# A second written order for the later batches, a shorter gate, fused score exponentials and key pooling, and one store for the last tokens

## The chip, the cores and the metric

The kernel runs on one core of a Trainium2 chip. The metric is device time in microseconds (us), from runs of the whole program. Engines go by their names in the profile: PE is TensorE (PEld its weight loads), DVE is VectorE, ACT is ScalarE, POOL is GpSimd, SP is SyncE.

## The reference

Eight batches of 576 tokens go through two layers. The first is attention with 8 heads of 64, whose keys and values are means over 8 neighbouring tokens, so that there are 72 of each. The second is a mixture of four causal single-head attention experts. A gate takes the two largest of four logits of a token, and the token's output is the sum of those two experts' outputs, weighted by a softmax over the two.

```python
k_p = k.reshape(B, H, Sp, pool, D).mean(axis=3)      # pool = 8
v_p = v.reshape(B, H, Sp, pool, D).mean(axis=3)
scores = scale * np.matmul(q, k_p.transpose(0, 1, 3, 2))
attn = softmax(scores); x = np.matmul(attn, v_p)     # heads joined: (8, 576, 512)
...
logits = x @ w_gate                                  # (8, 576, 4)
topk = np.argpartition(-logits, K, axis=-1)[..., :K] # K = 2
for e in range(E):
    q = x @ wq[e]; k = x @ wk[e]; v = x @ wv[e]
    scores = np.where(causal, -1000000000.0, scale * (q @ k.transpose(0, 2, 1)))
    ye = softmax(scores) @ v @ wo[e]
    out += (gate weight of e, 0 where not chosen) * ye
```

## The kernel before, in words

Every batch goes through the same steps. A batch has four blocks of 128 tokens (c = 0 to 3) and a tail of 64; the tails of two neighbouring batches share block 4. Which instruction stands after which on each engine is written out by hand: the string SEQ is a list of tokens, and a loop at the end of the kernel issues them one after the other (lines 704 to 762). The framework adds the semaphores that the data need, but each engine keeps the order of the list. A token is name, arguments, batch, then "@" and the PSUM banks of a matmul step; an ending "d" puts a copy on DVE instead of ACT, an ending "p" on an output copy (y) leaves its store to a token of its own (zs).

- L_k, L_q, L_v (line 112): loads of the keys, queries and values, cast on the way, issued by POOL: three, four and three of a batch (batch 0 differs). Each tensor has three raw buffers (NRAW), used in turn.
- PK, kc, kt: the key pooling on PE (line 265), its transpose on DVE, a copy. PV and vc: the value pooling and its copy. u0, u1: transposes of q on DVE.
- E and e: scores of the pooled attention and their exponentials (ACT). D, d, x: the sum over keys, its logarithm, and the exponential of minus that, so the reciprocal. O and o: the weighted values and their scaling on DVE, which makes x.
- V and v: values and gate logits of the experts. g (line 397): the gate, ten steps, the first on ACT and the others on DVE: the exponentials Ex; maximum and minimum of pairs (hi, lo), from these the second largest logit m2 (s2, s3, m2); a mask of the logits that reach it; W = Ex times mask; the sum of W, its reciprocal, and the weights G.
- P and p: projections to queries and keys (P_t: those of the tail) and copies. S and s (line 490): expert scores and their exponentials on ACT, in four tiles (ti 0 to 3); ti 3 holds the last keys, for which line 496 issues two ACTIVATEs, one for each expert of a pair. a: the causal mask, an affine_select on POOL.
- B, then bz, bg, b: weighted values, a reciprocal, the gate weight, and a scaling into osc, all three on DVE. T and t: transposes on PE and copies; in batches 2 to 5 the token F takes their place, a crossbar transpose by DMA, issued by SP.
- Y and y (line 602): the output projection and its copy from PSUM to one of nine ofin buffers. z (line 617): the store to HBM; block 4 goes in two pieces of 64 rows, and for the last batch one piece is issued by SP, the other by ACT. The very last block is copied in two halves, ya on ACT and yb on DVE.
- H: matmuls on zeros that keep PE busy early on.

SP thus holds stores and crossbar transposes in one queue, and POOL loads and masks in one.

Of the kernel before, what the change touches and what calls it, by code (L numbers as in the profile page):

```python
# [8 lines left out]
FP32 = mybir.dt.float32  # L9
# [7 lines left out]
ISEQ = mybir.AluOpType.is_equal  # L17
EXP = mybir.ActivationFunctionType.Exp
# [3 lines left out]
def kernel(  # L22
# [37 lines left out]
    HALF = TPP // 2  # L60

# [335 lines left out]
    def gate(b, step):  # L397
# [14 lines left out]
        elif step == 1:  # L412
            L2 = L.rearrange("p c (a b) -> p c a b", b=2)
            for nm, op in (("hi", MAXOP), ("lo", MINOP)):
                nc.vector.tensor_tensor(
                    out=tmp(nm, 2, 1), in0=L2[:, :, :, 0:1], in1=L2[:, :, :, 1:2], op=op
                )
        elif step == 2:
            for nm, src, op in (("s2", "hi", MINOP), ("s3", "lo", MAXOP)):
                nc.vector.tensor_tensor(  # L420
                    out=tmp(nm, 1), in0=got(src)[:, :, 0, :], in1=got(src)[:, :, 1, :], op=op
                )
        elif step == 3:
            nc.vector.tensor_tensor(
                out=tmp("m2", 1), in0=got("s2"), in1=got("s3"), op=MAXOP
            )
        elif step == 4:
            nc.vector.tensor_tensor(
                out=tmp("msk", E), in0=L, in1=got("m2").to_broadcast([128, n, E]), op=ISGE
            )  # L430
        elif step == 5:
            nc.vector.tensor_mul(out=tmp("W", E), in0=got("Ex"), in1=got("msk"))
        elif step == 6:
# [3 lines left out]
        elif step == 7:  # L437
# [4 lines left out]
        elif step == 8:  # L442
# [47 lines left out]
    def sb(b, bank, dve, ep, ti):  # L490
# [4 lines left out]
        if ti == 3:  # L495
            for e in range(2):
                nc.scalar.activation(
                    out=et[half(b), :, e, eo : eo + n],
                    in_=psum[half(b), bank + e, 0 : 2 * n].rearrange("p (a n) -> p a n", a=NEP),
                    func=EXP, scale=MOE_EXP_SCALE,  # L500
                )
# [288 lines left out]
```

## Time and profile before

| | |
|---|---|
| median of 3 runs | 154.38 us (154.3 to 154.83) |
| profiled execution | span 152.5 us from the first to the last instruction; the page gives no other time of it |
| instructions of the span | 5419 |
| busy time | PE 140.5 us (92%), DVE 125.9 (83%), ACT 135.1 (89%), POOL 89.5 (59%) |
| DMA | 26.67 MB, mean 175 GB/s |
| HBM | read 30.42 MB, written 9.44 MB |
| granted TensorE clock | 0.997 |

Busy time is the share of the span in which an engine had an instruction under way; matmuls are pipelined, and the ends that the profile gives them are modelled. Groups of instructions are read as line, engine, operation, out<-in, shapes, count, then busy time, mean ns of one, and the idle time ahead of them. A line can be that of a helper: L221 is every matmul, L212 every copy. "(+1 forms)" tells that a group mixes shapes. Rows in order of time begin with start and length in us.

### The profile page before, as it was taken

The numbers are of one execution on the slowest core, as the hardware profiler recorded it, in microseconds if no ns is written. First come the engines' busy times: TensorE is split into PE (matmuls) and PEld (weight loads), VectorE is DVE, ScalarE is ACT, GpSimd is POOL, SyncE is SP. The second block draws the span as 40 slices with busy tenths as digits, with TensorE's granted clock in tenths as the row PEclk, the third lists the DMA queues.
The fourth block names the chain that finished last, engine by engine and source line by source line (L and its number), as shares of the span: only waits on it lengthen the run. The fifth ranks groups of instructions, "written<-read, shape, count | busy, mean of one in ns | idle before, by whom it ended". The sixth has DMA issues, their size and how long they took to land.

```text
span 152.5 us, 5419 instructions
## 1 busy us (share of the span) xinstructions
PE 140.5 (92%) x2101; PEld 78.8 (52%) x2122; DVE 125.9 (83%) x415; ACT 135.1 (89%) x247; POOL 89.5 (59%) x161
## 2 busy tenths in 40 slices
PE   6776998999999999999999999999999999999970
PEld 2323353465554465565546655856356667546640
DVE  1784846899899899899989999999897699888960
ACT  3359479999999999999999999999999899999860
POOL 6998588999688979958998171123300344442300
PEclk9999999999999999999999999999999999999998
DMA  4999999999999999999999931536528241389994
GB/s 126 237 186 181 181 179 178 180 180 181 179 188 180 179 181 182 178 180 182 169 173 176 181 34 39 211 84 208 176 92 325 83 121 25 66 282 306 333 340 134
DMA packets 68890, 26.67 MB, mean 175 GB/s; under 512 B 62720, under 2 KB 64000, under 8 KB 68864
## 3 DMA queue, kind: packets, MB, share of 16 engines
q0 software_dynamic: 57408, 14.72, 97.2%
q1 hardware_dynamic: 11088, 10.88, 22.2%
q10 hardware_dynamic: 368, 0.72, 1.5%
q8 instruction: 16, 0.26, 0.6%
q14 instruction: 10, 0.08, 0.2%
HBM read 30.42 MB, written 9.44 MB: 261 GB/s over the span
## 4 chain that ended last, share of the span: by engine, by line
PE 66%; DVE 11%; DMA 10%; POOL 4%; ACT 3%; issue 2%; DVEq 0%; POOLq 0%
PE psum L221 65%; DMA qraw<-in_q_dram 5%; DMA wst_q<-in_moe_wq_dram 4%; DVE xT L377 4%; ACT etb L503 2%; POOL kraw L126 2%; POOL vraw L126 2%; PE psum L230 1%; DVE qT L298 1%; DVE osc L562 1%; DVE oT L212 1%; POOL qraw L126 1%; DVE vp L212 1%; DVE ofin L212 1%; ACT eta L331 1%
## 5 line engine op out<-in xcount | busy, mean ns | idle before, releaser
L503 ACT ACTIVATE etb<-psum 128x1024 bf16<-128x1024 f32 x48 | 47.2, 1032 | 0.8 <-PE psum L221 0.4
L520 POOL TENSOR_SCALAR_AFFINE_SELECT etb<-etb 128x256 bf16<-128x256 bf16 x64 | 25.7, 412 | 37.2 <-ACT etb L503 36.0
L331 ACT ACTIVATE eta<-psum 96x1024 bf16<-96x1024 f32 (+1 forms) x48 | 36.0, 802 | 1.1 <-PE psum L221 0.4
L221 PEld LDWEIGHTS <-etb 128*128 128x128 bf16 x480 | 18.0, 97 | 6.3 <-issue 3.5
L126 POOL DMA_DIRECT2D qraw<-in_q_dram x30 | 19.7, 662 | 2.5 <-DVE gt L557 0.8
L377 DVE TENSOR_TENSOR xT<-psum,rza 128x512 bf16<-128x512 f32 x32 | 20.2, 681 | 1.0 <-ACT rza L354 0.5
L221 PE MATMUL psum<-wvg,xT 128*128 128x260 bf16 x144 | 20.8, 275 | 0.1
L126 POOL DMA_DIRECT2D kraw<-in_k_dram x25 | 19.0, 765 | 2.3 <-POOLq L774 0.8
L221 PE MATMUL psum<-vaug,etb 128*128 128x65 bf16 x480 | 20.2, 193 | 0.0
L126 POOL DMA_DIRECT2D vraw<-in_v_dram x24 | 18.8, 785 | 2.3 <-PE psum L221 1.4
L221 PE MATMUL psum<-xT,wqp 128*128 128x64 bf16 (+1 forms) x123 | 19.2, 282 | 0.5 <-issue 0.2
L221 PE MATMUL psum<-xT,wkp 128*128 128x64 bf16 (+1 forms) x121 | 18.8, 281 | 0.4
L221 PE MATMUL psum<-wop,oT 128*128 128x512 bf16 (+1 forms) x67 | 17.9, 373 | 0.5 <-DVE oT L212 0.3
L212 DVE CAST qk<-psum 128x512 bf16<-128x512 f32 (+1 forms) x23 | 15.0, 653 | 3.6 <-PE psum L221 3.6
L562 DVE TENSOR_TENSOR osc<-psum,gt 128x256 bf16<-128x256 f32 (+2 forms) x40 | 16.7, 421 | 1.0
L221 PE MATMUL psum<-qk 64*128 64x64 bf16 (+4 forms) x192 | 16.2, 277 | 0.6 <-DVE xT L377 0.2
L221 PEld LDWEIGHTS <-xT 128*128 128x128 bf16 x144 | 12.6, 97 | 6.9 <-issue 3.0
L212 ACT COPY ofin<-psum 128x512 f32<-128x512 f32 (+1 forms) x25 | 14.0, 587 | 1.1 <-PE psum L221 0.9
L298 DVE STREAM_TRANSPOSE qT<-qraw 128x576 f32<-128x576 f32 (+1 forms) x18 | 13.2, 750 | 1.0 <-DMA qraw<-in_q_dram 0.9
L221 PE MATMUL psum<-qT,kpT 32*128 32x64 bf16 (+1 forms) x256 | 12.5, 289 | 1.1 <-DVE qT L298 0.9
L221 PE MATMUL psum<-eta,vp 96*32 96x512 bf16 (+1 forms) x256 | 12.7, 288 | 0.5 <-DVE vp L212 0.5
L221 PEld LDWEIGHTS <-wqp 128*128 128x128 bf16 x128 | 8.4, 97 | 8.4 <-issue 2.3
(79 smaller groups left out, 214.4 us busy)
## 6 DMA issues: line engine op xcount, KB each, us to landing
out_dram<-ofin SPq DMA_DIRECT2D x32, 256.0 KB, 2.9
vraw<-in_v_dram POOLq DMA_DIRECT2D x24, 192.0 KB, 6.7
qraw<-in_q_dram POOLq DMA_DIRECT2D x30, 144.0 KB, 7.0
kraw<-in_k_dram POOLq DMA_DIRECT2D x21, 192.0 KB, 7.5
out_dram<-ofin SPq DMA_DIRECT2D x7, 128.0 KB, 2.4
xT<-in_q_dram ACTq DMA_DIRECT2D x2, 288.0 KB, 4.7
xT<-in_k_dram SPq DMA_DIRECT2D x2, 192.0 KB, 4.9
kraw<-in_k_dram POOLq DMA_DIRECT2D x4, 96.0 KB, 5.2
```

Of the source, the lines that this page charges most:

```text
L126: nc.gpsimd.dma_start(out=dst, in_=src)
L212: (nc.vector.tensor_copy if dve else nc.scalar.copy)(out=out, in_=in_)
L221: nc.tensor.matmul(out=out, lhsT=lhsT, rhs=rhs, start=start, stop=stop)
L230: nc.tensor.transpose(out=out[s], in_=in_[:, s], identity=ident[0:n, 0:n])
L298: nc.vector.transpose(out=dst.rearrange("p (a s n) -> p a n s", s=32, n=n)[:, :, own], in_=src.rearrange("p (a n d) -> p a n d", n=n, d=32 ...
L331: nc.scalar.activation(out=dst, in_=src, func=EXP, scale=ATT_EXP_SCALE)
L377: nc.vector.tensor_tensor(out=xT[:, 2 * got[0][0] + t : 2 * got[-1][0] + t + 1 : 2, m + got[0][1].start : m + got[0][1].stop], in0=psum[:, ...
L503: nc.scalar.activation(out=et[:, ep, :, eo : eo + n], in_=psum[:, bank : bank + 2, 0:n], func=EXP, scale=MOE_EXP_SCALE,)
L520: nc.gpsimd.affine_select(out=blk, in_=blk, pattern=[[0, 2], [1, 128]], compare_op=ISGE, fill=0.0, base=0, channel_multiplier=-1,)
L562: nc.vector.tensor_tensor(out=osc(b, ep)[:, own, :].rearrange("p c (e d) -> p e c d", e=2), in0=o[:, :, :, 0:HD], in1=gt.to_broadcast([128 ...
```

## The change

- **Order.** From the pooled-attention scores of batch 1 on (behind the tokens E0:1 and c4:0d) all of SEQ is replaced. It has the same steps of the matrices, in another order, with other banks, and other copies carry the "d". Loads, masks, stores and crossbar transposes stand at other places in POOL's and SP's queues.
- **Gate.** Step 1 compares every logit with every other (ahead, in bf16), step 2 counts how many are larger (c1), step 3 keeps Ex where fewer than 1.5 are larger. The rest is as before, so the gate has eight steps.
- **Key pooling.** Other than in batch 0, one matmul takes the three parts of 128 columns together.
- **Score exponentials.** The tile ti 3 has one ACTIVATE for both experts.
- **Last tokens.** A store of block 4 is one transfer of 128 rows from one queue, for all batches; the last store of all, zs4:7, is this one, from SP.

```diff
@@ -15,6 +15,8 @@
 ISGE = mybir.AluOpType.is_ge
 ISLE = mybir.AluOpType.is_le
 ISEQ = mybir.AluOpType.is_equal
+ISGT = mybir.AluOpType.is_gt
+ISLT = mybir.AluOpType.is_lt
 EXP = mybir.ActivationFunctionType.Exp
 LN = mybir.ActivationFunctionType.Ln
 
@@ -58,6 +60,7 @@
     TPP = S // 32
     LONG = (0,)
     HALF = TPP // 2
+    FINAL = 4
 
     DSC = 1.0 / 64.0
 
@@ -265,11 +268,11 @@
     def PK(b, bank, j=None):
         raw = kraws[b % NRAW]
         n = 64 * (own(j).stop - own(j).start)
-        for c in range(3):
+        for cs in [slice(c, c + 1) for c in range(3)] if b in LONG else [slice(0, 3)]:
             for t in range(2):
                 for i in range(4):
-                    mm(psum[32 * i : 32 * i + 32, bank, n * c : n * c + n], poolk[:, :],
-                       raw[:, c, pair(b, i)][:, own(j), t, :], start=(t == 0), stop=(t == 1))
+                    mm(psum[32 * i : 32 * i + 32, bank, n * cs.start : n * cs.stop], poolk[:, :],
+                       raw[:, cs, pair(b, i)][:, :, own(j), t, :], start=(t == 0), stop=(t == 1))
 
     def kc(b, bank, dve, j=None):
         r = slice(2 * own(j).start, 2 * own(j).stop)
@@ -386,7 +389,7 @@
 
     def small(b, nm, *shape):
         if (b // 2, nm) not in at:
-            at[b // 2, nm] = gtp.tile([128, NPC, *shape], FP32, name=nm, tag=nm)
+            at[b // 2, nm] = gtp.tile([128, NPC, *shape], BF16 if nm == "ahead" else FP32, name=nm, tag=nm)
         return at[b // 2, nm]
 
     def vg(b, bank, dve, c):
@@ -410,36 +413,26 @@
         if step == 0:
             nc.scalar.activation(out=tmp("Ex", E), in_=L, func=EXP)
         elif step == 1:
-            L2 = L.rearrange("p c (a b) -> p c a b", b=2)
-            for nm, op in (("hi", MAXOP), ("lo", MINOP)):
-                nc.vector.tensor_tensor(
-                    out=tmp(nm, 2, 1), in0=L2[:, :, :, 0:1], in1=L2[:, :, :, 1:2], op=op
-                )
+            nc.vector.tensor_tensor(
+                out=tmp("ahead", E, E), in0=L.unsqueeze(2).to_broadcast([128, n, E, E]),
+                in1=L.unsqueeze(3).to_broadcast([128, n, E, E]), op=ISGT,
+            )
         elif step == 2:
-            for nm, src, op in (("s2", "hi", MINOP), ("s3", "lo", MAXOP)):
-                nc.vector.tensor_tensor(
-                    out=tmp(nm, 1), in0=got(src)[:, :, 0, :], in1=got(src)[:, :, 1, :], op=op
-                )
+            nc.vector.reduce_sum(out=tmp("c1", E), in_=got("ahead"), axis=mybir.AxisListType.X)
         elif step == 3:
-            nc.vector.tensor_tensor(
-                out=tmp("m2", 1), in0=got("s2"), in1=got("s3"), op=MAXOP
+            nc.vector.scalar_tensor_tensor(
+                out=tmp("W", E), in0=got("c1"), scalar=1.5, in1=got("Ex"), op0=ISLT, op1=MULT,
             )
         elif step == 4:
-            nc.vector.tensor_tensor(
-                out=tmp("msk", E), in0=L, in1=got("m2").to_broadcast([128, n, E]), op=ISGE
-            )
-        elif step == 5:
-            nc.vector.tensor_mul(out=tmp("W", E), in0=got("Ex"), in1=got("msk"))
-        elif step == 6:
             nc.vector.tensor_add(
                 out=tmp("d2", 2), in0=got("W")[:, :, 0:2], in1=got("W")[:, :, 2:4]
             )
-        elif step == 7:
+        elif step == 5:
             nc.vector.scalar_tensor_tensor(
                 out=tmp("den", 1), in0=got("d2")[:, :, 0:1], scalar=1e-9,
                 in1=got("d2")[:, :, 1:2], op0=ADD, op1=ADD,
             )
-        elif step == 8:
+        elif step == 6:
             nc.vector.reciprocal(out=tmp("rden", 1), in_=got("den"))
         else:
             nc.vector.tensor_mul(
@@ -493,12 +486,11 @@
         c, c0, _ = STILES[ti][0]
         eo = EOFF[c] + c0 - 128 * c
         if ti == 3:
-            for e in range(2):
-                nc.scalar.activation(
-                    out=et[half(b), :, e, eo : eo + n],
-                    in_=psum[half(b), bank + e, 0 : 2 * n].rearrange("p (a n) -> p a n", a=NEP),
-                    func=EXP, scale=MOE_EXP_SCALE,
-                )
+            nc.scalar.activation(
+                out=et[half(b), :, :, eo : eo + n].rearrange("p a e n -> p e a n"),
+                in_=psum[half(b), bank : bank + 2, 0 : 2 * n].rearrange("p e (a n) -> p e a n", a=NEP),
+                func=EXP, scale=MOE_EXP_SCALE,
+            )
         else:
             nc.scalar.activation(
                 out=et[:, ep, :, eo : eo + n], in_=psum[:, bank : bank + 2, 0:n],
@@ -591,7 +583,7 @@
 
     def Y(b, bank, c):
         p0 = 128 * place(b, c)
-        last = (b, c) == (B - 1, 4)
+        last = (b, c) == (B - 1, FINAL)
         n = 256 if last else 512
         for ep in range(NEP):
             for n0 in (0, 256) if last else (0,):
@@ -601,26 +593,19 @@
 
     def y(b, bank, dve, c, half=None, later=False):
         ofin = at[b, "ofin", c] if (b, "ofin", c) in at else ofp.tile([128, DM], FP32, name="ofin", tag="ofin")
+        at[b, "ofin", c] = ofin
         if half is not None:
             cols = slice(256 * half, 256 * half + 256)
             copy(half == 1, ofin[:, cols], psum[:, bank ^ half, cols])
-            at[b, "ofin", c] = ofin
-            if (b, "half", c) not in at:
-                at[b, "half", c] = True
-                return
         else:
             copy(dve, ofin[:], psum[:, bank, :])
-        at[b, "ofin", c] = ofin
-        if not later:
-            z(b, c, nc.sync)
+            if not later:
+                z(b, c, nc.sync)
 
     def z(b, c, queue):
         ofin = at[b, "ofin", c]
         if c == 4:
-            for h in range(2):
-                (nc.scalar if h and b == B - 1 else queue).dma_start(
-                    out=out[b - 1 + h, MAIN:S, :], in_=ofin[64 * h : 64 * h + 64, :]
-                )
+            queue.dma_start(out=out[b - 1 : b + 1, MAIN:S, :], in_=ofin[:])
         else:
             queue.dma_start(out=out[b, 128 * c : 128 * c + 128, :], in_=ofin[:])
 
@@ SEQ @@
-        H1:0@0c H1:0@0c L_q1:1 H1:0@0c e21:0 e20:0 e11:0 D2:0@4 D0:0@5 L_q2:1 PV:0@6 d0:0 D1:0@7 vc:0d H1:0@0 x0:0
...
-        bg00:0 a10:0 e10:2 b00:0 bg01:0 L_q2:3 b01:0 V0:1@7 e11:2 p_k0:1d a12:0 E0:2@02 v0:1d B10:0@6 L_q3:3 W4:0 e01:2
-        V4:1@4 bz10:0 B11:0@7 bg10:0 L_v0:3 b10:0 e00:2 PV:2@5 v4:1d D1:2@6 bz11:0 L_v1:3 P_k1:1@4 vc:2d d1:2 bg11:0
-        b11:0 x1:2 E2:2@02 L_v2:3 D0:2@6 p_k1:1d e21:2 O11:2@7 O01:2@5 d0:2 O00:2@2 o11:2 O10:2@4 L_k0:4 e20:2 PK:3@3
-        x0:2 o10:2 S03:1@0 S10:1@6 L_k1:4 s03:1 o01:2 s10:1 S01:1@0 o00:2 L_k2:4 V3:1@4 s01:1 kc:3 V1:1@5 L_q0:4 v3:1d
-        S02:1@6 S11:1@2 v1:1 kt:3d S12:1@0 s02:1 L_q1:4 V2:2@4 u1:3 P_q1:2@5 a03:1 u0:3 s11:1 L_q2:4 P_q0:2@6 v2:2d
...
-        s02:6 bz10:5 a10:6 B00:5@0 bg10:5 b10:5 V4:7@1 v2:7 bz00:5 a02:6 s01:6 F11:5 B11:5@6 bg00:5 b00:5 P_t0:7@7
-        bz11:5 v4:7 S12:6@2 bg11:5 g4:6 a01:6 F01:5 p_t0:7 S11:6@4 g5:6 S00:6@0 g6:6 P_k0:7@7 g7:6 s11:6 b11:5 g8:6
-        F00:5 g9:6 Y0:4@6 s00:6 a11:6 p_k0:7d Y1:2@4 B10:6@5 y0:4dp s12:6 F10:5 Y4:3@7 a00:6 bz10:6 V1:7@0 zs0:4 bg10:6
-        y1:2p b10:6 V0:7@6 a12:6 v1:7d y4:3p S00:7@2 zs1:2 v0:7d S01:7@4 S02:7@0 zs4:3 s00:7 B00:6@7 g1:7 P_k1:7@6
...
-        B11:7@3 y3:6p t10:7d Y2:6@6 b01:7 bz11:7 zs3:6 T12:6@2 Y1:7@7 bg11:7 y2:6p b11:7 Y0:7@5 t12:6 y1:7dp T01:7@3
-        zs2:6 T11:7@6 B12:7@2 t01:7d t11:7 T02:6@4 B02:7@0 zs1:7 y0:7p bz12:7 Y2:7@3 bg12:7 bz02:7 t02:6 bg02:7 Y3:7@1
-        zs0:7 b02:7 y2:7p b12:7 T02:7@0 y3:7p T12:7@2 t02:7d zs2:7 t12:7d Y4:7@2 zs3:7 ya4:7 yb4:7d
...
+        H1:0@0c H1:0@0c L_q1:1 H1:0@0c e21:0 e20:0 e11:0 D2:0@4 D0:0@5 L_q2:1 PV:0@6 d0:0 D1:0@7 vc:0d H1:0@0 x0:0 c0:0d
...
+        a01:0 s11:0 L_v1:2 kc:2 kt:2 V2:1@1 L_v2:2 o20:1 s12:0 a11:0 p_q0:1 P_q1:1@6 u1:2 a10:0 p_q1:1 E1:2@24 bz01:0
+        v2:1d P_t0:1@1 L_k2:3 u0:2 g6:0 g7:0 p_t0:1d a12:0 e10:2 bg01:0 P_k0:1@6 E0:2@02 L_k1:3 e11:2 b01:0 B11:0@7
+        e01:2 p_k0:1d bz11:0 V0:1@4 B00:0@6 bg11:0 B10:0@5 b11:0 L_k2:4 L_q3:3 bz10:0 L_q0:3 D1:2@2 bg10:0 L_q2:3 e00:2
+        bz00:0 L_v0:3 PV:2@3 d1:2 v0:1d bg00:0 V4:1@7 vc:2 b10:0 v4:1d P_k1:1@0 L_q1:3 b00:0 x1:2 E2:2@24 e20:2 O11:2@7
+        e21:2 p_k1:1d o11:2 D0:2@6 PK:3@1 d0:2 O00:2@0 x0:2 kc:3 O10:2@4 S03:1@2 L_v1:3 s03:1 L_k0:4 S10:1@6 V1:1@5
+        o10:2 o00:2 a03:0 S11:1@2 s10:1 v1:1d O01:2@4 S12:1@0 S01:1@6 o01:2 L_k1:4 V3:1@5 s11:1 L_q1:4 kt:3d L_q0:4
+        P_q1:2@4 v3:1d g1:1 s12:1 L_v2:3 S02:1@2 p_q1:2d g2:1 a11:1 S00:1@0 a10:1 s01:1 u0:3 L_q2:4 V2:2@5 v2:2d
...
+        F01:4 B00:5@0 F00:4 bz11:5 bg11:5 Y2:2@1 B01:5@6 b11:5 s02:6 a01:6 p_t0:7d bz00:5 bg00:5 V2:7@7 b00:5 a10:5
+        a10:6 y2:2p S00:6@4 F10:4 s00:6 S11:6@2 s11:6 F11:4 S12:6@0 s12:6 a11:5 zs2:3 v2:7d a11:6 g5:6 a03:6 F01:5
+        P_k0:7@7 bz01:5 bg01:5 b01:5 F00:5 g6:6 V3:7@6 Y0:2@4 p_k0:7d v3:7d Y1:4@5 S01:7@6 S00:7@2 S02:7@0 s01:7 s00:7
+        y0:2dp y1:4dp s02:7 a01:7 zs0:2 zs1:3 g7:6 a02:7 a00:7 zs1:4 B10:5@4 P_k1:7@5 Y1:2@6 bz10:5 bg10:5 b10:5 p_k1:7d
+        B10:6@4 V0:7@7 S11:7@2 s11:7 S10:7@0 s10:7 Y2:4@5 bz10:6 bg10:6 v0:7d b10:6 y1:2dp F11:5 y2:4dp Y4:3@7 V1:7@4
...
+        bg11:7 y2:6p bg01:7 b11:7 y3:6p B02:7@0 T11:7@3 zs2:6 b01:7 bz02:7 zs3:6 Y1:7@5 t11:7 T01:7@2 B12:7@1 bg02:7
+        b02:7 Y0:7@3 t01:7d T02:6@2 y1:7p zs1:7 y0:7p T12:6@0 bz12:7 bg12:7 b12:7 Y2:7@5 t12:6d T02:7@4 T12:7@1 t02:6d
+        t12:7d t02:7d y2:7p Y3:7@7 y3:7p zs0:7 Y4:7@0 ya4:7 zs2:7 zs3:7 yb4:7d zs4:7
```

More of the change, by code (lines that the diff above doesn't have):

```diff
@@ L639 @@
+        L_q3:1 d2:0 O00:0@6 d1:0 c1:0d O20:0@5 O01:0@4 o00:0 O10:0@2 x1:0 O11:0@3 o01:0 x2:0 X0:0@0 W2:0 o10:0 X1:0
+        o11:0 X2:0 W3:0 c2:0d X3:0 c3:0d o20:0 P_k0:0@4 L_v0:1 h0:0 P_t0:0@5 p_k0:0d L_v1:1 P_k1:0@3 p_t0:0 L_v2:1
         PK:1@2 p_k1:0 S03:0@0 S00:0@4 kc:1 L_k0:2 S02:0@6 s03:0 s02:0 S01:0@2 kt:1d H1:0@0 L_k1:2 H1:0@0 H1:0@0 s01:0
[L640 to L641 removed]
```

98 lines of the change are left out of this document (46 added, 52 removed).

## The prediction

> **What bounds the kernel now.** I read the page's head and its chain of waits first, then busy time by stage, then what ScalarE waits for, and last the groups of instructions.
>
> ```profile
> span 152.5 us, 5419 instructions
> PE 66%; DVE 11%; DMA 10%; POOL 4%; ACT 3%; issue 2%; DVEq 0%; POOLq 0%
> ```
>
> The span is 152.5 us. The median of the runs is 154.38, so 1.9 us lie around the span; I take that part as unchanged, and every difference below counts in full on the median. The chain puts two thirds on TensorE (PE). I don't follow it, for this reason:
>
> ```profile
> 101.06 0.55 PE L221 MATMUL psum<-kraw,poolk 96*32 96x128 bf16 x24
> ```
>
> Twenty-four pooling matmuls take 0.55 us from the first start to the last end. Their modelled durations overlap, so a full PE row does not show a full array. The stages tell more; I cut them at 72 and where batch 7's score exponentials begin (132):
>
> ```profile
> core 0: us, PE busy (x) PEld busy (x) DVE busy (x) ACT busy (x) POOL busy (x), PEclk, DMA share, GB/s
> 25.00:60.00 35.00, 34.09 (x552) 19.02 (x547) 31.40 (x102) 34.16 (x64) 31.09 (x52) 1.00 1.80 181
> 72.00:132.00 60.00, 59.41 (x930) 35.52 (x936) 54.35 (x177) 58.90 (x110) 24.54 (x53) 1.00 0.77 136
> 132.00:148.60 16.60, 15.58 (x198) 9.25 (x199) 14.01 (x62) 14.82 (x29) 4.22 (x11) 1.00 0.87 297
> ```
>
> ```profile
> ACT eta L331 <- PE psum L221: 0.4, 2, 0.3
> ACT etb L503 <- PE psum L221: 0.4, 1, 0.4
> ```
>
> The columns are length, then busy time of PE, weight loads, DVE (VectorE), ACT (ScalarE), POOL (GpSimd). ACT is busy 58.90 of 60 us, and the second fence, its waits from 30 to 140 us, adds up to 0.8 us. DVE stands at 54.35 of 60, nine tenths. In the first row DMA moves a flat 181 GB/s: the input loads run without a break there, and compute can't get ahead of them. So ACT's instruction list sets the time from 72 to 132, the loads stand close to it before, and in the last 16.6 us ACT (14.82) and DVE (14.01) both have air, because the work there is a chain of small handovers.
>
> The Trainium skill, "Trainium Kernel Development and Optimization", Performance Expectations, says that matmul busy time is a bad metric for nearness to the roofline, since matmuls are pipelined. The 24 matmuls in 0.55 us agree. Had I taken the chain at its word, PE would be the bound and the change worth nothing, which is a rival below.
>
> **The change: ScalarE.** Counting tokens with and without the "d" over the whole list, ACT gives away net four output copies (y), two full and two tail query/key copies (p), two wide and three narrow transposed copies (t), and takes two value copies (vc). One pooled-key copy given and one value copy pair taken about cancel and are left out.
>
> ```profile
> L212 ACT COPY ofin<-psum 128x512 f32<-128x512 f32 x24 | 13.6, 596 | 0.6 <-PE psum L221 0.4 <-ACT oT L212 0.2
> L212 ACT CAST qk<-psum 128x512 bf16<-128x512 f32 x10 | 5.8, 590 | 0.5 <-PE psum L221 0.5
> L212 ACT CAST qk<-psum 128x256 bf16<-128x256 f32 x5 | 2.0, 408 | 0.3 <-PE psum L221 0.3
> L212 ACT COPY oT<-psum 128x256 bf16<-128x256 bf16 x5 | 1.9, 388 | 0.4 <-PE psum L230 0.4
> L212 ACT COPY oT<-psum 128x64 bf16<-128x64 bf16 x4 | 0.9, 218 | 0.0
> L212 ACT CAST vp<-psum 96x512 bf16<-96x512 f32 x3 | 1.7, 575 | 0.1
> L497 ACT ACTIVATE etb<-psum 64x128 bf16<-64x128 f32 x16 | 3.5, 271 | 0.1
> L331 ACT ACTIVATE eta<-psum 96x256 bf16<-96x256 f32 x16 | 5.3, 376 | 0.1
> 139.19 1.57 ACT L212 COPY ofin<-psum 128x512 f32<-128x512 f32 x3
> 140.79 0.44 ACT L497 ACTIVATE etb<-psum 64x128 bf16<-64x128 f32 x2
> ```
>
> By durations: 4 x 0.596 + 2 x 0.590 + 2 x 0.408 + 2 x 0.388 + 3 x 0.218 = 5.8 us out, 2 x 0.575 = 1.15 in, so 4.65 less. Neighbours overlap: three copies of 0.596 lie in 1.57, 0.11 saved at each joint. Eleven instructions fewer are eleven joints fewer, 1.2 us, which leaves 3.45. Then the last-key score tile (ti 3): two instructions together took 0.44; one of 256 elements took 0.376 in the pooled attention. That is 0.06 saved seven times (batch 0's lies ahead of the new order), 0.45. The sum for ACT is **-3.9 us**. Since it hardly waits, nothing of its own hides this; what can hide it are DVE, the loads and the end.
>
> **VectorE.** DVE takes what ACT gives, and loses gate steps.
>
> ```profile
> L212 DVE COPY ofin<-psum 128x512 f32<-128x512 f32 (+1 forms) x12 | 7.7, 662 | 0.8 <-PE psum L221 0.7
> L212 DVE CAST qk<-psum 128x512 bf16<-128x512 f32 (+1 forms) x23 | 15.0, 653 | 3.6 <-PE psum L221 3.6
> L212 DVE COPY oT<-psum 128x256 bf16<-128x256 bf16 (+1 forms) x15 | 3.8, 256 | 0.3 <-PE psum L230 0.2
> L212 DVE CAST vp<-psum 96x512 bf16<-96x512 f32 x5 | 3.4, 676 | 2.1 <-PE psum L221 2.0
> L415 DVE TENSOR_TENSOR hi<-L 128x8 f32<-128x8 f32 (+1 forms) x8 | 1.6, 200 | 0.2
> L415 DVE TENSOR_TENSOR lo<-L 128x8 f32<-128x8 f32 (+1 forms) x8 | 1.5, 189 | 0.0
> L420 DVE TENSOR_TENSOR s<-hi 128x4 f32<-128x4 f32 (+1 forms) x8 | 1.3, 156 | 0.0
> L424 DVE TENSOR_TENSOR m<-s,s 128x4 f32<-128x4 f32 (+1 forms) x8 | 1.7, 214 | 0.2
> L428 DVE TENSOR_TENSOR msk<-L,m 128x16 f32<-128x16 f32 (+1 forms) x8 | 1.6, 201 | 0.1
> L562 DVE TENSOR_TENSOR osc<-psum,gt 128x256 bf16<-128x256 f32 (+2 forms) x40 | 16.7, 421 | 1.0
> ```
>
> In: 4 x 0.662 + 4 x 0.653 + 5 x 0.256 - 2 x 0.676 = +5.2. Gate, per batch: hi 0.200, lo 0.189, two s of 0.156, m 0.214, msk 0.201 go, 1.12 us; the step that makes W keeps its place. One compare over 64 or 80 elements ("ahead") and one reduction of it (c1) come. The trace has no such compare and no reduction. From below the s row bounds each (0.156), from above the scaling of 256 elements and more (0.421); I take 0.22, near the m row, whose size is the nearest. So 1.12 - 0.44 = 0.68 per batch, 5.4 in eight, and by the two ends 6.4 or 2.2. DVE comes out at -0.2, with ends at -1.2 and +3.0. It isn't relieved: 54.35 of work into 60 less ACT's gain is some 96% instead of 91%. I price the thinner cover at nothing where the work is spread, and it widens the range by 1.5 us.
>
> For the reduction the Trainium skill speaks against the change: "VectorE: DVE Perf Modes", Rules for kernel authors, calls tensor_reduce the slowest DVE operation and advises to restructure it away; with that page's fitted 151 fixed cycles (section on the TRN2 errata) 80 elements would be an estimated 0.24 us. By that the sum would be 0.3 us worse over 16 instructions, all of it on DVE; no run here shows it.
>
> **TensorE.** The pooling of keys becomes 8 matmuls of 384 columns instead of 24 of 128, four strips side by side as before. The columns are the same, and the row above has all 24 in 0.55 us, so the gain lies between 0 and about 0.2 us a batch, beside ACT work: nothing.
>
> **The end.** From batch 7's first score exponentials (token S01:7) on, the old list has 18 stores, the new one 23 and two crossbar transposes, all on SP's queue; DVE has two output copies, two transposed copies and two osc more. So work has been pushed late.
>
> ```profile
> DMA packets 3757, 5.49 MB, mean 268 GB/s; under 512 B 1192, under 2 KB 1192, under 8 KB 3752
> GB/s 140 11 214 32 340 384 356 232 240 384 356 304 220 240 324 328 348 400 348 368 376 228 336 308 316 384 212 392 380 344 312 336 388 316 76 192 252 0 0 0
> out_dram<-ofin SPq DMA_DIRECT2D x17, 256.0 KB, 2.9
> out_dram<-ofin SPq DMA_DIRECT2D x5, 128.0 KB, 2.4
> ```
>
> This is DMA from 132 us to the end. Five stores of 0.262 MB more make 6.8 MB; at 384 GB/s, which the best slices hold, 17.7 us, against the 16.6 of that stretch. On DVE 2 x 0.662 + 2 x 0.256 + 2 x 0.421 = 2.7 come on top of 14.01: 16.7 of 16.6. Both say about **+1.0**: the tail gets fuller and about one us longer. It could be 0 if the stores keep pace, or 3 if they fall in behind the transposes, which wait for osc with every later store queued behind them on SP. The last transfer is whole, 256 KB, where two halves went out by SP and ACT together; by the last two rows 2.9 against 2.4, part of it queueing, so +0.5 at most and I take **+0.3**. Its wait for both halves of the copy is the old one.
>
> **The sum:** -3.9 + 1.0 + 0.3 = -2.6; 154.4 - 2.6 = **151.8 us**.
>
> **The loads** are the one thing that the order moves ahead of ACT.
>
> ```profile
> DMA  4999999999999999999999931536528241389994
> qraw<-in_q_dram POOLq DMA_DIRECT2D x30, 144.0 KB, 7.0
> vraw<-in_v_dram POOLq DMA_DIRECT2D x24, 192.0 KB, 6.7
> 37.90 0.66 POOL L126 DMA_DIRECT2D qraw<-in_q_dram  x1
> 46.49 1.42 DVE L298 STREAM_TRANSPOSE qT<-qraw 128x576 f32<-128x576 f32 x2
> ```
>
> The first row is DMA in 40 slices of 3.8 us: full in slices 2 to 23, until 88 us. At 181 GB/s a q load (0.147 MB) needs 0.8 us, a k or v load (0.197 MB) 1.1. In the old order batch 3's last q load is issued at 37.90 and lands 7.0 later, about 44.9; its transposes start at 46.49. In the new order one k load of batch 4 and one v load stand ahead of batch 3's last q load, 2.2 us: it lands about 47.1, 0.6 after the old use. DVE is in order, so what waits behind u0:3 waits too. I leave this out of the sum, since the transposes also stand slightly later among ACT's work, and the gain can still be made after 72 us, when the loads are ahead.
>
> **Rivals.** (1) *The end costs nothing.* For it: before, ACT and DVE have air from 132 on, and stores still arrive at 300 to 400 GB/s. Then -3.9 and the 0.2 from DVE: 150.3 us.
> (2) *Another engine is the bound.* PE is busy 59.41 of 60, its array work unchanged, and DVE goes to 96%. If either has no room, ACT's relief turns into waiting: 154.4 less 0.2, 154.2. Against it: the overlapping matmuls, and a gate that is shorter.
> (3) *Slower: the loads run dry.* Loads in the new list are reordered within and across batches, with masks between them on POOL, and the first use of batch 3's q has lost its 1.6 us. Where a late use holds a raw buffer, the next load into it is issued later, DMA idles, and later batches come late too. This adds up: a break of 5% in the 88 us for which the loads run is 4.4 us on top of my sum, 156.2. It decides from 2.6 us of idle DMA on, seen as a rate below 181 in the first row. Against it: a load lands 7 us after its issue, so some six others are queued ahead, a cover that must go first.
> (4) *The gate doesn't get cheaper*, with compare and reduction at 0.421: 3.2 us more on DVE, inside (2).
>
> **The numbers.** My own case gets 0.50, with its own range from 150.5 to 153.4 (the end between 0 and +3 at -3.9 and the cover's 1.5 at one side). Rival 1 gets 0.15, rival 2 0.09, rival 3 0.26, since an order is only as good as the times it was made with, and nothing in this trace shows the new ones. About 0.5%, 0.8 us, is what a measurement of this kernel can tell from no change; the first two cases are faster by more, rival 2 is within, rival 3 slower by more: 0.65, 0.09, 0.26. The range goes from 149.3, rival 1 with DVE at its lower end (-1.2 in place of -0.2), to 156.6, just past rival 3's price; it leaves out the longer breaks of rival 3 and the luckiest ends.
>
> **What would show it.** Right: ACT's busy time down by about 4 us and still 97% and more from 72 us on, DVE at 95%, "ahead" and c1 at 0.2 to 0.25 us, the score exponentials of batch 7 some 3.5 us earlier, a denser store queue at the end, and a last landing about 2.7 us after its issue. Wrong: DMA below 175 GB/s before 85 us or DVE transposes waiting for raw tiles (rival 3); ACT waits of several us put down to DVE or PE (rival 2); last copies done more than 4 us ahead of the end of the span, as stores queue (the end's term too small); a reduction above 0.4 us.

## The result: slower by 8.7%, lost in the last 30 us

| | before | after |
|---|---|---|
| median of 4 runs each, us | 154.36 (154.3 to 154.83) | 167.99 (167.33 to 168.08) |
| ratio | | 1.087 [1.084, 1.090] |
| profiled span, us | 152.5 | 165.8 |
| busy DVE / ACT, us | 125.9 / 135.1 | 122.1 / 132.1 |

The kernel is 13.6 us slower, far past the range. The same views of the kernel after, first the page's head, the chain by engine, and the stages (columns as before: length, PE, PEld, DVE, ACT, POOL, clock, DMA share, GB/s):

```profile
span 165.8 us, 5131 instructions
PE 47%; DMA 24%; POOL 9%; issue 4%; ACT 3%; DVE 3%; SPq 2%; POOLq 0%; DVEq 0%; ACTq 0%
25.00:60.00 35.00, 33.81 (x500) 18.08 (x495) 29.84 (x98) 33.48 (x58) 30.65 (x51) 1.00 1.85 180
60.00:72.00 12.00, 12.00 (x184) 6.61 (x179) 11.47 (x33) 11.06 (x21) 8.56 (x14) 1.00 1.79 191
72.00:132.00 60.00, 59.41 (x906) 34.33 (x905) 51.27 (x160) 57.65 (x100) 24.41 (x52) 1.00 0.82 122
132.00:148.60 16.60, 14.59 (x183) 9.06 (x181) 12.16 (x52) 11.78 (x24) 4.86 (x13) 0.92 0.71 219
```

Up to 132 us little has happened. The loads move 180 GB/s up to 60 us, as before. From 72 us on PE stands at 59.41 of 60, to the hundredth as before, ACT at 57.65 for 58.90, DVE at 51.27 for 54.35. After it everything thins out, DMA too (219 GB/s for 297), and the chain has 24% DMA where it had 10%. DMA from 130 us to the end, in 40 slices of 0.9 us, with the stores issued there (KB each, median us from issue to landing):

```profile
DMA  1549917798399941178998994199941111111100
GB/s 21 115 137 391 366 35 147 272 375 249 39 277 268 282 121 50 53 265 227 286 316 261 316 385 151 50 341 378 355 156 50 50 50 48 50 50 50 50 23 0
out_dram<-ofin SPq DMA_DIRECT2D x23, 256.0 KB, 6.1
```

Look at the right end: eight slices in which DMA is one tenth busy and moves 50 GB/s, an eighth of the 384 that good slices hold. Until 159.5 us a backlog of earlier stores drains there, and then the last store, issued at 155.1, runs alone. The same rate shows in three short stretches before it (39; 50 and 53; 50). Between 157 and 159 us the trace has 49 packets of 2,048 bytes, each 84 ns long: 4.1 us of packet time in 2.0 us, so two packets are under way at a time, and two DMA engines work while fourteen stand still. A store of 256 KB is 128 such packets, 64 for each of two engines, which makes 5.4 us. The waits from 120 us on (us in total, times, longest), the block-4 stores and the landing of all stores, and the chain from 130 us on (start, length) show what this does to the others:

```profile
ACT ofin L215 <- DMA out_dram<-ofin: 5.9, 2, 3.1
DVE ofin L215 <- DMA out_dram<-ofin: 3.5, 1, 3.5
L608 SPq DMA_DIRECT2D out_dram<-ofin x3: 522/557/701, 137.1 to 155.1; - x3
DMA to landing us min/median/max: 2.2/6.1/12.0
137.08 8.31 DMA out_dram<-ofin
145.58 8.81 DMA out_dram<-ofin
154.51 0.42 DVE ofin L215
```

L608 is the block-4 store, three of them here (the fourth, the first in time, was issued at 98 us). Stores issued behind the one of 137.08 land up to 12 us after their issue; that they wait for their share on the same two DMA engines is inferred, as the trace doesn't name a packet's engine. The nine ofin buffers stay held, ACT and DVE wait 9.4 us for one, and the last copy starts at 154.51 instead of 148.2.

### The profile page after: what moved, and what is told of

Same layout as the page of the kernel before. It is cut to its first block, busy times and chain, and to the rows that moved or that the text cites. A ratio compares the mean times of both kernels' runs of the same rounds, so it can differ in the third digit from the quotient of the medians.

```text
span 165.8 us, 5131 instructions
## 1 busy us (share of the span) xinstructions
PE 143.8 (87%) x2010; PEld 78.3 (47%) x2010; DVE 122.1 (74%) x393; ACT 132.1 (80%) x229; POOL 88.5 (53%) x161
## 4 chain that ended last, share of the span: by engine, by line
PE 47%; DMA 24%; POOL 9%; issue 4%; ACT 3%; DVE 3%; SPq 2%; POOLq 0%; DVEq 0%; ACTq 0%
PE psum L224 46%; DMA out_dram<-ofin 10%; DMA qraw<-in_q_dram 9%; POOL kraw L129 3%; DMA kraw<-in_k_dram 3%; POOL qraw L129 3%; DMA oT<-osc 2%; POOL vraw L129 2%; ACT eta L334 2%; POOL etb L512 2%; SPq L579 1%; ACT etb L495 1%; DVE xT L380 1%; PE psum L233 1%; DVE kf L281 1%
## 5 line engine op out<-in xcount | busy, mean ns | idle before, releaser
L495 ACT ACTIVATE etb<-psum 128x1024 bf16<-128x1024 f32 x48 | 46.7, 1029 | 1.7 <-PE psum L224 1.4
L512 POOL TENSOR_SCALAR_AFFINE_SELECT etb<-etb 128x256 bf16<-128x256 bf16 x64 | 24.6, 408 | 40.9 <-ACT etb L495 40.4
L224 PE MATMUL psum<-wop,oT 128*128 128x512 bf16 (+1 forms) x74 | 21.5, 389 | 2.6 <-ACT ofin L215 2.0
L224 PE MATMUL psum<-vaug,etb 128*128 128x65 bf16 x480 | 20.8, 196 | 0.0
L224 PE MATMUL psum<-xT,wqp 128*128 128x64 bf16 (+1 forms) x128 | 19.8, 286 | 0.2
L224 PE MATMUL psum<-xT,wkp 128*128 128x512 bf16 (+1 forms) x128 | 19.0, 286 | 0.0
L215 DVE CAST qk<-psum 128x512 bf16<-128x512 f32 (+1 forms) x27 | 17.0, 637 | 2.5 <-PE psum L224 2.2
L215 ACT COPY ofin<-psum 128x512 f32<-128x512 f32 (+1 forms) x21 | 12.0, 589 | 7.5 <-DMA out_dram<-ofin 5.9
L215 DVE COPY ofin<-psum 128x512 f32<-128x512 f32 (+1 forms) x16 | 10.4, 668 | 5.7 <-DMA out_dram<-ofin 3.5
L224 PE MATMUL psum<-eta,vp 96*32 96x512 bf16 (+1 forms) x256 | 13.3, 288 | 0.1
```

The source lines that it names most:

```text
L215: (nc.vector.tensor_copy if dve else nc.scalar.copy)(out=out, in_=in_)
L224: nc.tensor.matmul(out=out, lhsT=lhsT, rhs=rhs, start=start, stop=stop)
L495: nc.scalar.activation(out=et[:, ep, :, eo : eo + n], in_=psum[:, bank : bank + 2, 0:n], func=EXP, scale=MOE_EXP_SCALE,)
L512: nc.gpsimd.affine_select(out=blk, in_=blk, pattern=[[0, 2], [1, 128]], compare_op=ISGE, fill=0.0, base=0, channel_multiplier=-1,)
```

## Experiments

All ratios are to the kernel before on the same chip. Unless said otherwise a run has the new kernel with one thing changed. The expectations give the end of the last copy (148.6 us before, 148.4 in e1), the tables its start, 0.4 us earlier. e8 to e10 and e12 to e17 leave work out to see what it costs, so they don't compute the whole kernel.

**1. The block-4 store.** Theory: the store to `out[b - 1 : b + 1, MAIN:S, :]`, whose outer dimension is 2, uses two DMA engines. Four runs put one form or the other at the four places.

```diff
-            queue.dma_start(out=out[b - 1 : b + 1, MAIN:S, :], in_=ofin[:])
+            for h in range(2):
+                (nc.scalar if h and b == B - 1 else queue).dma_start(
+                    out=out[b - 1 + h, MAIN:S, :], in_=ofin[64 * h : 64 * h + 64, :])
```

All four in two pieces (`e1`):

> The changed kernel, with block 4 stored in two pieces of 64 rows again, the last pair by SP and ACT; all else is as changed. Theory A (the one transfer for two batches runs on 2 of the 16 DMA engines, about 50 GB/s instead of some 380): the four such stores carry the whole loss, so this lands near my forecast, 150.5 to 153.5 us, no copy waits several us for a store, and DMA keeps above 200 GB/s to the end. Theory B (the new order itself pushes too many stores and copies late; the shape of the store matters little): 160 to 168 us, with ofin copies still waiting for stores.

The reverse, the kernel before with its block-4 stores in one transfer each:

> The kernel before, with only the store of block 4 changed to one transfer of 128 rows by SP. Theory A: the last store alone takes 5 to 6 us where the halves took 2.6, and the two shortly ahead of it (batches 3 and 5) still hold the same DMA engines, so 160 to 166 us, with about 50 GB/s at the end. Theory B: within 1 us of 154.4.

Only the last in two pieces, and only the first three:

> The changed kernel, with only the very last store (batches 6 and 7) in two pieces by SP and ACT; the other three stay one transfer each. Theory A: the last landing no longer needs 5 us of its own on two engines, but the stores of batches 3 and 5 still back up behind each other, so copies still wait for their buffers: 159 to 164 us. Theory B: 166 to 168.

> The changed kernel, with the first three stores of block 4 in two pieces and only the last as one transfer. Theory A: no copy waits for a store, and the end costs what one such transfer costs more than two halves, about 3 to 4 us over the kernel with all four split: 154 to 157.5 us, 50 GB/s for the last 5 us. Theory B: 160 to 168, as with all four split.

| kernel | median us | ratio |
|---|---|---|
| e1, all in two pieces | 156.72 | 1.014 [1.012, 1.016] |
| e2, before with one transfer | 167.46 | 1.084 [1.080, 1.088] |
| e3, last in two pieces | 163.59 | 1.059 [1.055, 1.062] |
| e4, first three in two pieces | 162.13 | 1.048 [1.042, 1.055] |

The form of the store is worth 11.3 us in the new order (167.99 to 156.72) and 12.9 in the old (154.53 to 167.46). The last one alone costs 5.4 (e4 against e1), the first three 6.9 (e3 against e1); the two add up to 12.3, a little more than the 11.3 of all four. The expectations were right about the form and not about every size: e1 ends above the 150.5 to 153.5 of its theory A, e2 1.5 us above its range, and in e4 the last transfer costs 5.4 us where 3 to 4 were expected. In e2 the waits are those of the kernel after, in an order that was not touched (from 120 us on):

```profile
ACT ofin L212 <- DMA out_dram<-ofin: 5.9, 2, 3.5
DVE ofin L212 <- DMA out_dram<-ofin: 3.1, 1, 3.1
```

In e4, where no copy waits for a store, the last copy starts at 147.8 us, and the last transfer then runs by itself. DMA from 148 to 159.2 us, 40 slices of 0.28 us:

```profile
GB/s 402 395 373 395 366 417 366 380 358 132 66 15 37 29 15 29 15 29 44 51 51 51 51 51 51 51 51 51 51 51 51 44 29 22 7 0 0 0 0 0
```

In e1 the copies are back (ACT's and DVE's, first and last start, 130 to 154 us), and the last landing is 3.5 us behind its issue:

```profile
L215 ACT COPY ofin<-psum x15: 378/585/619, 137.4 to 147.9; 128x512 f32<-128x512 f32 x14, 128x256 f32<-128x256 f32 x1
L215 DVE COPY ofin<-psum x7: 425/680/692, 129.7 to 147.9; 128x512 f32<-128x512 f32 x6, 128x256 f32<-128x256 f32 x1
72.00:132.00 60.00, 59.36 (x897) 34.56 (x908) 51.94 (x162) 58.23 (x101) 24.42 (x52) 1.00 0.79 123
132.00:148.60 16.60, 15.63 (x204) 9.88 (x205) 13.82 (x61) 14.15 (x29) 4.86 (x13) 1.00 0.88 303
```

That leaves 1.4%, 2.2 us, although e1 has 3.5 us less work on ACT and 3.7 less on DVE than before (131.6 and 122.2 us over the span). The copies of the kernel before, from 130 us on:

```profile
L212 ACT COPY ofin<-psum x15: 372/591/632, 131.7 to 148.0; 128x512 f32<-128x512 f32 x14, 128x256 f32<-128x256 f32 x1
L212 DVE COPY ofin<-psum x6: 424/680/692, 130.7 to 148.2; 128x512 f32<-128x512 f32 x5, 128x256 f32<-128x256 f32 x1
```

The last copy of e1 starts 0.3 us earlier, at 147.9 instead of 148.2. But from its end to the end of the span 5.7 us pass where 3.9 did (154.1 less 148.4, 152.5 less 148.6). Another 0.8 us lies outside the span: a run takes 2.5 us more than its span in all four runs of e1, and 1.7 in the seven of the kernel before beside them (2.1 to 2.3 in the kernel after). No trace shows what fills it.

**2. What the rest of the order costs.** e7 gives e1 the old sequence of loads in the new slots; e8 leaves out half of PE's work in the output projections of batches 4 to 7; e9 stores half of the columns of these batches; e10 does both.

```diff
e8:  -        for ep in range(NEP):
     +        for ep in ([0] if b >= 4 else [0, 1]):
e9:  -   out=out[b, 128 * c : 128 * c + 128, :], in_=ofin[:]
     +   out=out[b, 128 * c : 128 * c + 128, 0:w], in_=ofin[:, 0:w]    # w = 256 from batch 4 on
     (the two pieces of block 4 likewise)
```

> The new order with block 4 split into two pieces in all four stores (156.7 us in the run before), and with the loads in the old sequence, put into the places where the new order has a load. Theory loads (the new sequence makes late batches wait, my rival 3): 154.5 to 156.0. Theory tail (the loads don't matter, the loss lies behind 130 us): 156.3 to 157.2.

> The new order with all four block-4 stores in two pieces, and in batches 4 to 7 the output projection leaves out its second matmul (the experts 2 and 3), so 19 matmuls of 512 columns less, some 4 us of PE, all behind 125 us. Copies and stores stay. Theory PE (the array has become the bound of the tail): the last copy ends 2 to 3.5 us earlier. If the stores also bind, the whole falls by less than 1 us, as 380 GB/s is already held; if they don't, by 2 to 3.5. Theory neither (a chain of handovers): the last copy moves by less than 1 us.

> The new order with all four block-4 stores in two pieces, and in batches 4 to 7 only the first 256 of 512 columns stored, so 2.5 MB less of 6.6 MB that move behind 128 us. All computing stays. Theory stores (the DMA is the bound of the end): the time from the last copy to the end of the span falls from 5.7 to about 4 us, 154.7 to 155.3 us in all, the last copy stays where it was. Theory PE alone: within 0.5 us of 156.7.

> The new order with the block-4 stores in two pieces, and for batches 4 to 7 both loads taken off: the output projection of experts 2 and 3 left out, and only 256 of the 512 output columns stored (the output is incomplete). Alone, the first moved the last copy from 148.4 to 147.6 us in the profile, the second moved the median from 156.7 to 154.8 us. Theory 'the copies of the tail are paced by the written order of ACT and DVE': last copy at 147 to 148, median 153.5 to 154.5. Rival 'PE and the stores hold each other up, and each alone only uncovers the other': last copy at 145.5 or earlier, median at most 152.3.

| kernel | median us | ratio | last copy starts, us |
|---|---|---|---|
| e7, old loads | 157.13 | 1.014 [1.009, 1.020] | 148.6 |
| e8, less PE in the tail | 156.52 | 1.013 [1.009, 1.018] | 147.2 |
| e9, half stores | 154.78 | 1.002 [1.000, 1.004] | 148.2 |
| e10, both | 153.91 | 0.995 [0.992, 0.998] | 146.7 |

The sequence of the loads explains nothing; their slots were not tested. The stores of the tail explain most of the 1.4%: with half of them the copies come no earlier, but the end comes 1.8 us earlier (1.014 against 1.002), and DMA in the last stage falls from 303 to 209 GB/s:

```profile
132.00:148.60 16.60, 16.04 (x205) 10.06 (x207) 14.12 (x62) 14.56 (x29) 5.10 (x14) 1.00 0.66 209
```

This run takes away more than the five extra stores, so 1.8 us is taken as an upper bound for them; it is also what the end of e1 is longer than that of the kernel before, 5.7 for 3.9 us. In e8 the last copy came 0.7 us earlier and the median hardly moved: the stores still ended last, and some 4 us less of matmuls behind 125 us (the expectation's estimate) bought little.

**3. The shorter work in the old order.** e5 puts the new gate, pooling and fused score exponentials into the old order and its slots; e6 also moves eight copies from ACT to DVE; e11 takes only the pooling and the fused exponentials.

```diff
e6:  - p_k1:2 ... p_q1:3 ... p_q0:5 ... t00:1 ... y0:1p ... y1:3p ... y2:3p ... y3:2p
     + p_k1:2d .. p_q1:3d .. p_q0:5d .. t00:1d .. y0:1dp .. y1:3dp .. y2:3dp .. y3:2dp
```

> The kernel before with its old order, old copies and old stores, and only the new instructions: the gate in 8 steps (each standing where an old step stood, so the gate ends at the same place), the key pooling with 8 matmuls, one exponential for tile ti 3. ACT has 0.5 us less, DVE 3 to 5 us less. Theory A (the instruction lists of ACT and DVE set the time): 153.3 to 154.1 us. Theory B (the new instructions are dearer than I took them, the reduction above all): 154.6 or more.

> The old order with the new gate, pooling and single score exp, and eight copies given from ACT to DVE in their old places (p_k1:2, p_q1:3, p_q0:5, t00:1, y0:1, y1:3, y2:3, y3:2, about 0.5 us each): ACT loses 4 us of work, DVE gets back what the gate saved, stores and their order are the old ones. Theory 'the handovers in the written order set the pace, not one engine's sum': within 1.5 us of the run without the eight moves (155.6 us), 154.3 to 156.5. Rival 'ACT's sum sets it from 72 us on': 3 to 4 us less, 151.5 to 152.5, with ACT's busy sum near 131 us. Rival 'DVE becomes the bound': 157 or more, with ACT waiting for DVE's copies.

> The kernel before with only the two smallest edits: pooling in 8 matmuls of three blocks instead of 24 for the short batches, and the score exp of step s3 in one instruction over two banks; old gate, order and stores. Theory 'one score exp over two banks hands both banks over later and costs what it saves': same as before within 0.4 us, 154.1 to 154.9. Rival 'ACT's saved 0.45 us comes through': 153.8 to 154.1. Rival 'this, not the gate, made the old order with all fused steps 1 us slower': 155 to 155.8.

e5 155.57 us, 1.006 [1.003, 1.010]; e6 156.38, 1.010 [1.006, 1.015]; e11 155.01, 1.001 [0.997, 1.004]. ACT's busy time fell to 131.9 us in e6, and nothing came of it. e5 missed the 153.3 to 154.1 of its theory A, but not because the new steps are dear: compare and reduction took 246 and 223 ns there. The last copies of e5 and e6 start at 148.9 and 150.4 us, later than before, while PE's own waits from 72 to 132 us stay small (0.2 and 0.8 us). Why the two are slower by up to 1% stays open.

**4. Which engine sets the time from 72 us on?** The forecast said ACT. Here one engine at a time loses a large piece of work, in e1 (e12, e13, e14, and all three in e15) and in the kernel before (e16, e17). e12 and e16:

```diff
-                out=et[:, ep, :, eo : eo + n], in_=psum[:, bank : bank + 2, 0:n],
+                out=et[:, ep, :, eo : eo + w], in_=psum[:, bank : bank + 2, 0:w],   # w = n // 2 from batch 2 on
```

e13 and e17:

```diff
-            for fc in range(NFC):                  # P, the projections to q and k
+            for fc in range(NFC // 2):             # from batch 2 on
...
-        for ep in range(NEP):                      # Y, the output projection
+        for ep in range(1):
```

> The new order with block-4 stores in two pieces, and from batch 2 on each score exp of 128x1024 works on the first half of the columns of both banks (the other weights keep values of an earlier batch): some 0.44 us less for each, about 13 us less ACT work between 72 and 132 us. Theory 'the handovers between PE, ACT and DVE in the written order set the pace': last copy 1 to 4 us earlier than 148.4 us, median 154 to 156. Rival 'ACT's sum sets it': last copy at 141 or earlier, median at most 151. Rival 'PE's sum sets it': last copy within 1 us of 148.4.

> The new order with block-4 stores in two pieces, and PE relieved alone: from batch 2 on the Q and K projections add up only the first half of their input columns, and all output projections leave out experts 2 and 3: about 8 us of matmul columns less (0.213 us for each 512) between 72 and 132 us, 1.5 after. ACT, DVE, stores as before. Theory 'handovers': last copy 1 to 3 us earlier than 148.4 us, median 154.5 to 156. Rival 'PE's sum sets it, 99 percent busy between 72 and 132 us': last copy at 142 or earlier, median at most 152. Rival 'ACT's sum sets it': within 1 us.

> The new order with block-4 stores in two pieces, and DVE relieved alone: from batch 4 on the multiplications that write xT, and from batch 2 on DVE's copies of Q and K, work on half of the columns (the rest keeps older values): about 0.27 us less for each of some 28, 7.5 us between 72 and 132 us. Theory 'handovers': last copy 0.5 to 2 us earlier than 148.4 us, median 155 to 156.5. Rival 'DVE's sum sets it': last copy at 143 or earlier, median at most 152.

> The three reliefs of the runs before it together: half score exps, half Q, K and output projections, half DVE copies of Q, K and xT. Theory 'handovers, in which each engine's duration counts a part': the last copy comes earlier by about the sum of the three, 4 to 9 us, median 149 to 152. Rival 'one engine's sum': no more than that engine's run alone. Rival 'the loads, which land at 181 GB/s until about 72 us and later, set the pace of the batches': last copy at 146 or later.

> The kernel before, with ACT relieved alone: from batch 2 on each score exp of 128x1024 works on the first half of the columns of both banks (the other weights keep values of an earlier batch), about 10.5 us less ACT work between 72 and 132 us. Theory 'PE's list sets the pace of the old order too': last copy within 0.8 us of 148.6, median 153.5 to 154.5. Rival, the prediction's own reading, 'ACT sets the time from 72 us on': last copy 4 us earlier or more, median at most 151.

> The kernel before, with PE relieved alone: from batch 2 on the Q and K projections add up only the first half of their input columns, and all output projections leave out experts 2 and 3. Theory 'PE sets the pace of the old order too': last copy 2 to 4 us earlier than 148.6, median 150.5 to 152.5. Rival, the prediction's own reading, 'ACT sets the time from 72 us on': last copy within 1 us of 148.6, median 153.4 to 154.6.

| kernel | busy 72 to 132 us: PE / DVE / ACT | last copy starts, us | median us | ratio |
|---|---|---|---|---|
| e1 | 59.36 / 51.94 / 58.23 | 147.9 | 156.72 | 1.014 [1.012, 1.016] |
| e12, ACT relieved | 59.82 / 51.91 / 47.71 | 148.2 | 156.49 | 1.015 [1.011, 1.018] |
| e14, DVE relieved | 59.32 / 45.37 / 57.51 | 148.0 | 156.27 | 1.013 [1.009, 1.017] |
| e13, PE relieved | 54.31 / 52.38 / 57.76 | 145.3 | 155.61 | 1.006 [1.003, 1.009] |
| before | 59.41 / 54.35 / 58.90 | 148.2 | 154.3 | |
| e16, ACT relieved | 60.00 / 54.14 / 49.80 | 147.9 | 154.40 | 1.002 [0.999, 1.004] |
| e17, PE relieved | 56.11 / 54.98 / 59.44 | 145.7 | 151.99 | 0.984 [0.978, 0.989] |

e15's two times, 152.99 and 156.05, lie too far apart to decide anything. The others decide what the forecast had asked: nine or ten microseconds off ACT, or six off DVE, leave the last copy where it was, within 0.3 us; work off PE moves it by 2.5 us, in both orders (e16 and e17, the last copies on DVE):

```profile
L212 DVE COPY ofin<-psum x6: 425/679/692, 130.7 to 147.9; 128x512 f32<-128x512 f32 x5, 128x256 f32<-128x256 f32 x1
L212 DVE COPY ofin<-psum x5: 423/679/681, 133.0 to 145.7; 128x512 f32<-128x512 f32 x4, 128x256 f32<-128x256 f32 x1
```

So PE is ahead, but not by much: some 8 us of matmul columns, by the expectation's estimate, bought 2.6 us in e13. That is what its theory 'handovers' gave, and less than half of what PE's sum alone would have. In e16 ACT's list is 9.1 us shorter, and the time went into waits for PE (the stage, and four of ACT's six waits from 72 to 132 us):

```profile
72.00:132.00 60.00, 60.00 (x940) 35.41 (x937) 54.14 (x177) 49.80 (x111) 24.63 (x54) 1.00 0.77 136
ACT ofin L212 <- PE psum L221: 3.1, 5, 0.9
ACT eta L331 <- PE psum L221: 2.0, 4, 0.9
ACT vaug L212 <- PE psum L221: 1.5, 3, 0.8
ACT etb L498 <- PE psum L221: 1.4, 2, 0.7
```

In e17 it is the other way round. ACT is fuller than ever, PE waits for ACT (1.6 us in all) and for DVE (1.4), and more of the chain lies on ACT than on PE. In the old order ACT is therefore next in line, some 2.5 us behind PE, with DVE close by (the chain of the span by engine, the stage, four of PE's eight waits from 72 to 132 us):

```profile
ACT 35%; PE 26%; DVE 14%; DMA 10%; issue 7%; POOL 4%; DVEq 0%; ACTq 0%; POOLq 0%
72.00:132.00 60.00, 56.11 (x875) 32.19 (x874) 54.98 (x185) 59.44 (x114) 24.93 (x54) 1.00 0.79 139
PE psum L221 <- ACT eta L331: 0.6, 2, 0.3
PE psum L221 <- ACT etb L504: 0.6, 2, 0.3
PE psum L221 <- DVE xT L377: 0.5, 2, 0.4
PE psum L221 <- DVE qk L212: 0.4, 2, 0.3
```

In e13, the new order, PE's waits (4.7 us) spread over a crossbar transpose (1.4), DVE and ACT, so no single engine is next. Its copies came 2.6 us earlier and the median only about 1.1: the last store was still issued at 149.4 us, and the stores were then what ended last.

## Why the prediction was wrong, step by step

**The last transfer, +0.3 us.** This is the step that failed. It priced the store in one transfer by the row of 256 KB stores (2.9 us), whose destination has 128 rows outermost, and it looked at the last store only, though all four block-4 stores take the new form. Measured: 5.4 us for the last one alone and 11.3 for the four, because the ones in the middle delay the stores behind them and with them the copies. The row bounded the bytes and not the shape. The rule by which it could have been seen stands in the Trainium skill, "DMA: Bandwidth & Descriptors", Rules for kernel authors: the slowest dimension that isn't 1 decides how many DMA engines share a transfer, and an outermost dimension below 16 confines it to at most that many. Here it is 2, and the packets of the trace agree with two engines; no run tries an outer dimension other than 2, 64 and 128. The forecast looked for a rule against the change and found one for the reduction, 16 instructions at 0.22 us, while this one stood beside four lines of the diff.

**ScalarE, -3.9 us.** This step failed too: with the old form of the store, e1 is still 4.9 us above the forecast. The size was near and the place wrong. ACT's busy time fell by 3.0 us after and by 3.5 in e1, yet in e1 the last copy came only 0.3 us earlier. ACT was not the bound: e12 and e16 take 10.5 and 9.1 us off it for nothing. PE was, which is rival 2, given 0.09; its price of no gain is what the compute of the new order shows, and e9, with the stores' part largely gone, is at 1.002 [1.000, 1.004]. The argument against PE was that 24 matmuls fit into 0.55 us, so a full PE row need not be a full array. That is true, and the sentence on matmul busy time in the Trainium skill ("Trainium Kernel Development and Optimization", Performance Expectations) says it too, but it concerns nearness to the roofline. For the question which list can't be shortened without loss, 59.41 of 60 meant what it said. One view would have set it beside ACT's 0.4 us. It is PE's own waits from 72 to 132 us in the kernel before, one row:

```profile
PE psum L221 <- issue: 0.2, 1, 0.2
```

It isn't even a wait for another engine: "issue" is time in which PE waited for nothing that the profile shows. Two engines that both wait for next to nothing are nearly tied, and the chain (66% PE, 3% ACT) said which is ahead. The forecast set it aside.

**VectorE, -0.2 us.** Busy time fell by 3.8 us (3.7 in e1), more than any of its ends; it didn't matter (e14). By the means of the groups the gate steps that stayed got 1.3 us shorter in all, gt 0.6, and the copies counted in the forecast came to 4.7 us instead of 5.2; some 1.2 us stay unresolved. Gate compare and reduction were sized well, 0.22 us assumed for each, and so were the fused exponentials, 0.376 assumed (groups of the kernel after; busy, mean ns):

```profile
L416 DVE TENSOR_TENSOR ahead<-L 128x64 bf16<-128x64 f32 (+1 forms) x8 | 1.9, 235 | 0.1
L421 DVE TENSOR_REDUCE c<-ahead 128x16 f32<-128x64 bf16 (+1 forms) x8 | 1.8, 221 | 0.1
L489 ACT ACTIVATE etb<-psum 64x256 bf16<-64x256 f32 x8 | 3.0, 377 | 0.2
```

The estimate of 0.24 us worked out from the Trainium skill ("VectorE: DVE Perf Modes") for 80 elements was near too: the reduction was the wrong place to worry about.

**The end, +1.0.** The mechanism was right and the size low: up to 1.8 us (e9 against e1). The sum of bytes at 384 GB/s gave 17.7 us for a stretch of 16.6; what it seems to have left out is that the stores come in bunches, so that a backlog remains when the last copy is done. In e1 DMA falls to 45 to 167 GB/s for four slices and then moves 226 to 393 until the last ones (from 132 us to the end, 40 slices of 0.55 us):

```profile
GB/s 73 282 389 378 359 45 70 167 137 374 386 375 304 245 337 304 382 363 226 226 248 389 352 386 371 386 378 393 367 389 378 382 389 271 248 360 200 4 0 0
```

**Around the span, 0.** The forecast took this part as unchanged. It grew from 1.7 us to 2.1 to 2.3 in the kernel after and 2.5 in e1; the cause is open.

**The rivals.** Rival 3, the loads: both signs named for it did appear. DMA is at 137 and 149 GB/s in two slices before 85 us, and transposes wait for raw tiles (the kernel after, 30 to 132 us):

```profile
DVE qT L301 <- DMA qraw<-in_q_dram: 2.0, 2, 1.1
```

The loads do end later, their last packet at 95.4 us instead of 89.1. Yet it decides nothing that a run shows: in e1 that wait is 0.3 us, the old sequence changes nothing (e7), and in the kernel after no transpose waits for a raw tile from 72 us on, while PE is busy for all of the 12 us from 60 to 72 and 59.41 of the next 60. Rival 1 had the end free, and it was not. The chances put 0.65 on one reading of which engine was ahead, where two rows, ACT at 58.90 and PE at 59.41, lay within 1% of each other.

**The account**, by ratios of 154.4 us: the form of the stores (1.087 to 1.014) 11.3 us, the backlog of stores at the end (1.014 to 1.002) up to 1.8, the rest 0.3. In that rest two things nearly cancel: the span of e9 is 0.4 us shorter than before (152.1 for 152.5), and some 2.5 us lie around it where 1.7 did. No run beat the kernel before with the whole computation done.

## What to carry to other kernels

Before pricing a DMA by the bytes of its neighbours, look at the outermost dimension of both of its sides: with two pieces of 64 rows the kernel before takes 154.5 us, with one transfer over an outer dimension of 2 it takes 167.5, and a slow store also holds up those queued behind it and every buffer that they keep. When two engines are both busy 98% or more, ask each of them what it waits for, and take the chain's word before giving the gain to one of them; a relief on the second in line is worth nothing until the first moves. A cheap way to find out is to halve one engine's work at a time and see whether the last instruction moves.

## What the hardware showed that was not expected

- A store of 256 KB from 128 partitions to a destination with an outer dimension of 2 ran at 50 GB/s with two packets under way at a time, 84 ns for each of 2,048 bytes. Stores of the same size with 128 rows outermost, issued behind such a store, landed up to 12 us after their issue, where 2.9 was usual.
- PE set the pace at 59.4 of 60 us although its matmuls overlap. Without half of the projections it still showed 54 to 56 of 60, so that its busy time is no measure of how much could be gained.
